# Attention's k^T v with four tokens of all heads on a partition: 40 matmuls of 128 rows in place of 72 of 64, for batches 3 to 7

## The chip, the cores and the metric

The kernel runs on one core of one Trainium2 chip. The metric is the device time of one execution in microseconds (us); the time of a kernel is the median of its runs. A profile of one execution goes with it. It shows five engines: PE (TensorE matmuls; its weight loads are listed as PEld), DVE (VectorE), ACT (ScalarE), POOL (GpSimd) and SP (SyncE, which here only issues DMAs). L237 means line 237 of the kernel before.

## The reference

Two stages follow each other, on 8 batches, 8 heads, 576 tokens and a head dimension of 64, all in float32.

```python
def phi(x, c, s):
    r = np.maximum(x, 0.0)
    return np.concatenate([r * c, r * s], axis=-1)      # 64 -> 128 features
q_p = phi(q, cos_w, sin_w)      # cos_w, sin_w depend on the token's position alone
k_p = phi(k, cos_w, sin_w)
kv = np.einsum('bhsf,bhsd->bhfd', k_p, v)               # 128 x 64 for each head
z = np.sum(k_p, axis=2)
num = np.einsum('bhsf,bhfd->bhsd', q_p, kv)
den = np.einsum('bhsf,bhf->bhs', q_p, z)[..., None] + 1e-06
x = num / den                                           # tokens x (8 heads * 64)
h = x @ w_in                                            # 512 -> 2048
g = h * (1.0 / (1.0 + np.exp(-1.702 * h)))
return g @ w_out                                        # 2048 -> 512
```

The matmuls run in bfloat16 with float32 sums.

## The kernel before

**The work of a batch.** From k and v the kernel forms k^T v for each head, a 128 x 65 matrix: 128 features by 64 columns of v and one column of ones, which gives the sum z of the denominator. q's features are transposed by DMA (L219) into qT. For each chunk of 128 tokens (the fifth has 64) eight matmuls, one a head, multiply qT with k^T v (`num_mm`, L310); DVE divides (`num_div`, L321 to L325), and a DMA transposes the quotient into x (L354). Then come 16 groups of four matmuls of 128 x 512 (`mm1`, L365), each group followed by a gelu on ScalarE (L371), and the product with w_out, written as seven Strassen-Winograd products of 16 matmuls each (`wino_mm`, L516). The last chunk of 64 tokens of each batch is left for a stage at the end.

**The layout of k and v.** `src_of` (L57) puts nine consecutive tokens on a partition and two heads above each other: 64 partitions hold one head's 576 tokens and the other 64 hold those of the next head, for four pairs of heads. A partition's piece in DRAM is 9 x 64 x 4 = 2304 bytes long, 512 such pieces a tensor. `load_kv` (L146) issues one DMA for k and one for v on SP.

`kv_operands` (L874) makes the matmul operands on DVE: for each of nine tokens two instructions (`trig`, L169: relu times cosine and relu times sine) on 128 x 256 elements, 18 in all, and from batch 3 on one cast of v to bfloat16 (`vcopy`, L193) on 128 x 2304.

The matmuls of k^T v (`kv_mm`, L232 to L238) contract the 64 partitions of one head, nine times with one token each:

```python
for i in range(i0, i1):                # pairs of heads
    for j in range(NS):                # NS = 9
        for hh in range(2):
            r = slice(hh * 64, hh * 64 + 64)
            nc.tensor.matmul(st["kv", i][:, hh, ds(col, n)], kr[r, j, i, :], rhs(r, i, j),
                             start=(j == 0), stop=(j == NS - 1))
```

That is 72 matmuls of 64 rows and 65 columns, alternating between the lower and the upper half of the array. `kv_evac` (L245) copies the result from PSUM to the tile kvs on DVE.

**q's layout.** From batch 1 on q is loaded differently (`load_chunks`, L127): four consecutive tokens of all eight heads on each of 128 partitions (pieces of 1024 bytes, 1024 of them) and the last 64 tokens on 64 partitions (512 pieces of 256 bytes), in two DMAs. `trig_q` (L176) makes each chunk's features with two instructions of 128 x 512, or 64 x 512 for the fifth chunk (L185).

**The order of the work.** All of it is written out by hand. In the loop at L886, block b runs batch b's `mm1` and Winograd products and prepares batch b + 1. At `fc` 0 DVE gets q's ten `trig_q` instructions and SP five transposes; at `fc` 1 `kv_operands` follows and SP issues the load of q of batch b + 2. At `fc` 12 DVE gets five sums for the Winograd products: two of s3 (L474), then s1, s2 and s4 (L470, L472, L476). At `fc` 14 PE does `kv_next` (L708): the 72 matmuls, and the eviction on DVE behind those sums. After `fc` 15 `x_next` (L880) runs chunk after chunk between the Winograd products. Once the fourth chunk's transpose is issued, SP gets `load_kv` for batch b + 2 (L933), and then the transpose of x's fifth chunk. Block 1 is arranged differently (its k^T v, for batch 2, comes after its `mm1`). GpSimd issues the DMAs of the output (L522), each of which waits for its sums on DVE or ACT. SP and GpSimd work through their lists in order.

**Borrowed places.** The batch 0 copy of v (`vb`) lies in the tile `sums`, and the end stage puts its sums into kr, kf, vf, qn and qf when these are done. The tile `warm` (zeros for matmuls that fill waits at the start) and `row` (batch 0's column sums) have places of their own.

Of the kernel before, what the change touches and what calls it, by code (L numbers as in the profile page):

```python
# [9 lines left out]
F32 = mybir.dt.float32  # L10
BF16 = mybir.dt.bfloat16
# [9 lines left out]
def kernel(  # L21
# [9 lines left out]
    nc = tc.nc  # L31
    B, H, S, D = q.shape
    d_model = H * D
    d_ff = moe_w_in.shape[1]
    KC = d_model // 128
    FC = d_ff // 128
    NS = S // 64
    MT = 512
    NI = H // 2

    const = ctx.enter_context(tc.tile_pool(name="const", bufs=1))
    one = ctx.enter_context(tc.tile_pool(name="one", bufs=1))
# [3 lines left out]
    small = ctx.enter_context(tc.tile_pool(name="small", bufs=3))  # L46
    pmm = ctx.enter_context(tc.tile_pool(name="pmm", bufs=4, space=PSUM))
    pat = ctx.enter_context(tc.tile_pool(name="pat", bufs=2, space=PSUM))
# [8 lines left out]
    def src_of(src, b, i0=0, i1=NI):  # L57
        return src[b, 2 * i0:2 * i1].rearrange("(i hh) (p j) d -> (hh p) i (j d)", hh=2, j=NS)

    qf = one.tile([128, 2560], F32, name="qf")  # L60
    kf, vf = [one.tile([128, NI, S], F32, name=n) for n in ("kf", "vf")]
    sums = one.tile([128, 4, d_ff], BF16, name="sums")
    vb = sums.rearrange("p n e -> p (n e)")[:, 0:NI * S].rearrange("p (i e) -> p i e", i=NI)
    qf0 = qf[:, 0:NI * S].rearrange("p (i e) -> p i e", i=NI)
    for t, src, cut in ((kf, k, 192), (qf0, q, 256)):
# [10 lines left out]
    nc.gpsimd.memset(ident, 1.0)  # L76
    nc.gpsimd.affine_select(out=ident, in_=ident, compare_op=mybir.AluOpType.is_equal,
                            fill=0.0, base=0, pattern=[[-1, 128]], channel_multiplier=1)
    warm = const.tile([128, 512], BF16)
    nc.vector.memset(warm, 0.0)  # L80
    pos_f = const.tile([128, NP], F32)
    nc.vector.tensor_copy(pos_f, pos_i)
# [22 lines left out]
    nc.scalar.activation(gl, halfpi, AF.Gelu_apprx_sigmoid)  # L105

    VW = 66
    wsum = one.tile([128, 4, d_ff], BF16, name="wsum")
    kr = one.tile([128, NS, NI, 128], BF16, name="kr")
    vt = one.tile([128, NS, NI, VW], BF16, name="vt")  # L110
    qn = one.tile([128, 5, H, 128], BF16, name="qn")
    qn0 = qn.rearrange("p c h f -> p (c h f)")[:, 0:NS * NI * 128].rearrange(
        "p (j i f) -> p j i f", j=NS, i=NI)
    qT = one.tile([128, H, 640], BF16, name="qT")
# [9 lines left out]
    def load(t, src, b, eng=nc.gpsimd):  # L124
        eng.dma_start(out=t, in_=src_of(src, b))

    def load_chunks(t, src, b, eng):  # L127
        eng.dma_start(out=t[:, 0:2048].rearrange("p (h e) -> p h e", h=H),
                      in_=src[b, :, 0:512, :].rearrange("h (p c) d -> p h (c d)", c=4))
        eng.dma_start(out=t[0:64, 2048:2560].rearrange("p (h e) -> p h e", h=H),  # L130
                      in_=src[b, :, 512:S, :].rearrange("h p d -> p h d"))

    def load_q(b, eng=nc.gpsimd):
        load_chunks(qf, q, b, eng)
# [5 lines left out]
    def wcol(kc, fc):  # L140
# [2 lines left out]
        w = w_in_t[g][:, kc, :] if g < 2 else w_in_t[2][:, kc, ts(g - 2, 512)]  # L143
        return w.rearrange("p (f c) -> p f c", c=4)[:, :, c]

    def load_kv(b):  # L146
        load(kf, k, b, nc.sync)
        load(vf, v, b, nc.sync)

    def load_wout(g):  # L150
        nc.gpsimd.dma_start(out=w_out_sb[:, ts(g, 4), :], in_=wout_r[g])
# [9 lines left out]
    def trig(dst, src, j, act=False, eng=nc.vector):  # L161

        i = src[:, :, ts(j, 64)]
        for cs, w in enumerate((cosw, sinw)):
            o = dst[:, j, :, ts(cs, 64)]
            if act is True or (act == "sin" and cs == 1):
                nc.scalar.activation(o, i, AF.Relu, scale=w[:, j:j + 1])
            else:
                eng.tensor_scalar(o, i, 0.0, w[:, j:j + 1], op0=MAX, op1=MUL)  # L169

    def chunk(t, c):
        if c < 4:
            return t[:, 0:2048].rearrange("p (h c d) -> p c h d", h=H, c=4)[:, c]
        return t[0:64, 2048:2560].rearrange("p (h d) -> p h d", h=H)

    def trig_q(c, act=False):  # L176
        n = 128 if c < 4 else 64
        i = chunk(qf, c)
        for cs, w in enumerate((cosw, sinw)):
            o = qn[0:n, c, :, ts(cs, 64)]  # L180
            sc = w[0:n, NS + c:NS + c + 1]
            if act:
                nc.scalar.activation(o, i, AF.Relu, scale=sc)
            else:
                nc.vector.tensor_scalar(o, i, 0.0, sc, op0=MAX, op1=MUL)  # L185

    def vcopy(i0=0, i1=NI, act=False):
        o = vt[:, :, i0:i1, 0:64].rearrange("p j i e -> p i j e")
        i = vf[:, i0:i1].rearrange("p i (j e) -> p i j e", e=64)
        if act:  # L190
            nc.scalar.activation(o, i, AF.Copy)
        else:
            nc.vector.tensor_copy(o, i)  # L193

    tps = {}

# [25 lines left out]
    st = {}  # L222
# [9 lines left out]
    def kv_mm(i0, i1, rhs, col, n):  # L232
        for i in range(i0, i1):
            for j in range(NS):
                for hh in range(2):
                    r = slice(hh * 64, hh * 64 + 64)
                    nc.tensor.matmul(st["kv", i][:, hh, ds(col, n)], kr[r, j, i, :], rhs(r, i, j),  # L237
                                     start=(j == 0), stop=(j == NS - 1))  # L238

    def kvs_of(h):  # L240
        return st["kvs"][:, h % 2, h // 2, 0:65]

    def kv_evac(i0, i1, n=65):
        o = st["kvs"][:, :, i0:i1, 0:n]
        nc.vector.tensor_copy(o, st["ps", i0].rearrange("p hh (i e) -> p hh i e", e=n))  # L245
# [6 lines left out]
                         start=first, stop=last)  # L252

    def ksum_rows():
        st["row"] = small.tile([2, 512], BF16, name="row", bufs=1)
        nc.vector.tensor_copy(st["row"], st["ks"][0:2])

    def ksum_turn():
# [27 lines left out]
    def div_half(a):  # L286
        pv = nums["ps"][a][:, 0:260].rearrange("p (h e) -> p h e", h=4)
        inv = small.tile([128, 4], F32, name="invh")
        nc.vector.reciprocal(inv, pv[:, :, 64])
        xn = small.tile([128, 4, 64], BF16, name="xh")  # L290
        nc.vector.tensor_tensor(xn, pv[:, :, 0:64],
                                inv.unsqueeze(2).to_broadcast([128, 4, 64]), op=MUL)
        nums[0, a] = [nums["ps"][a], xn]
# [79 lines left out]
    def mm1(b, fc):  # L373
        mm1_part(b, fc, 0, MT)
        gelu(fc)
# [78 lines left out]
    def tail_blk(i, qd):  # L454
# [1 line left out]
        return gt[:, ts(qd, 4), ts(i, 256)]  # L456

    tail_flat = [t.rearrange(f"p {r} -> p ({r})")[:, 0:2 * d_ff].rearrange("p (n f t) -> p n f t", n=2, f=HF)
                 for t, r in ((kr, "j i f"), (qT, "h t"))]
    tail_sg = {n: tail_flat[i // 2][:, i % 2] for i, n in enumerate(("s1", "s2", "s3", "s4"))}  # L460
    MAIN, TAIL = (main_blk, sg), (tail_blk, tail_sg)

# [130 lines left out]


    ws = {}
    for t, names in ((kf, ("s1", "s2")), (vf, ("s3", "s4"))):
        both = t.rearrange("p i e -> p (i e)")[:, 0:2048].bitcast(BF16).rearrange(
            "p (n k f) -> p n k f", n=2, k=2)
        for i, n in enumerate(names):
            ws[n] = both[:, i]  # L600
# [103 lines left out]
    def kv_mm_next():  # L704
        kv_open()
        kv_mm(0, 4, vt_rhs, 0, 65)

    def kv_next():  # L708
        kv_mm_next()
        kv_evac(0, 4)  # L710
# [161 lines left out]
    start_block(1)  # L872

    def kv_operands(b):  # L874
        for j in range(NS):
            trig(kr, kf, j, act="sin" if b == 2 and j % 2 else False)
        if b > 2:
            vcopy()

    def x_next(b, c):  # L880
        num_mm(c)
# [4 lines left out]
    for b in range(1, B):  # L886
        nb = b + 1 if b + 1 < B else None
        if nb is None:
            break
        f0 = 5 if b == 1 else 0  # L890
        for fc in range(f0, FC):
            if nb is not None and fc == f0:
                for c in range(5):
                    trig_q(c)
                    qturn_dma(c)
            if nb is not None and fc == f0 + 1 and b > 1:
                kv_operands(nb)

                if nb + 1 < B:
                    load_q(nb + 1, nc.sync)  # L900
            if fc == 8 and b == 1:
                load_q(nb + 1, nc.sync)
                g_sums(("s3",), 0)
                g_sums(("s3",), 1)
                kv_operands(nb)
            if fc == 12:
                if b > 1:
                    g_sums(("s3",), 0)
                    g_sums(("s3",), 1)
                g_sums(("s1", "s2", "s4") if b > 1 else ("s1", "s2"), 0)  # L910
            if fc == 13 and b == 1:
                vcopy()
            if fc == 14 and nb is not None and b > 1:
                kv_next()
            mm1(b, fc)
        if nb is not None:
            x_open(nb)
            if b > 1:
                x_next(nb, 0)
            g_sums(("s1", "s2"), 1)  # L920
            at = ({2 * p + 1: [p + 1 if nb < B - 1 else (4, 1, 2, 3)[p]] for p in range(4)} if b > 1 else
                  {3: [0], 4: [1], 5: [2], 6: [3], 8: [4]})
            wino_open()
            for p in range(7):
                for c in range(2):
                    wino_mm(p, c)
                    s = 2 * p + c
                    if c == 1:
                        wino_after(b, p)
                    for c2 in at.get(s, ()):  # L930
                        x_next(nb, c2)
                        if c2 == 3 and nb + 1 < B:
                            load_kv(nb + 1)  # L933
                    if s == 1 and b > 1:
                        g_sums(("s4",), 1)
                    if s == 1 and b == 1:
                        kv_mm_next()
                        kv_evac(0, 4)
                        g_sums(("s4",), 0)
                    if s == 6 and b == 1:  # L940
                        g_sums(("s4",), 1)
# [3 lines left out]
    b = B - 1  # L945
# [100 lines left out]
```

## Time and profile before

| what | us |
|---|---|
| median of 3 runs | 278.96 |
| the runs | 278.21, 278.96, 280.12 |
| the profiled execution | 281.36 |
| its span, first to last instruction | 279.6 |
| PE busy | 268.8 |
| DVE busy | 198.4 |
| ACT busy | 135.1 |
| POOL busy | 41.4 |

The granted clock of TensorE is 0.998 of full speed. Busy times of the engines lie beside each other and are not added up: an engine that isn't the one waited for costs nothing. Matmuls are pipelined: a matmul of 65 columns is listed with 0.19 us, but the next starts some 0.03 us behind it, so PE's time is read from the distance of starts. The DVE instructions overlap in the same way. Where a DMA is listed with a time to landing, it runs from the issue to the signal that all of it has arrived.

### The profile page before, as it was taken

What the parts mean: (1) busy time and instruction counts of PE and PEld (TensorE: products, weight loads), DVE (VectorE), ACT (ScalarE), POOL (GpSimd) and SP (SyncE); (2) the same over time, 40 slices, a digit from 0 to 9 for tenths busy, and PEclk for the clock granted to TensorE, in tenths of its full rate; (3) what the DMA queues carried; (4) which work ended last, traced back from release to release, by engine and by line L of the source; (5) the groups of instructions that cost most, each with busy time, mean ns of one, the idle gap of its engine ahead of it and who ended that gap; (6) DMA issues with size and microseconds to landing.
All of it is one profiled execution on the core that took longest, in us unless ns stands there. A gap on an engine that the chain in (4) does not pass through costs nothing.

```text
span 279.6 us, 6701 instructions
## 1 busy us (share of the span) xinstructions
PE 268.8 (96%) x2727; PEld 195.0 (70%) x2748; DVE 198.4 (71%) x474; ACT 135.1 (48%) x241; POOL 41.4 (15%) x70
## 2 busy tenths in 40 slices
PE   7899999997999999999999999999999999999994
PEld 2685645844885589558955896589657976899984
DVE  4943776469886985987598759876887783654741
ACT  6967552657116521662156215631464147577621
POOL 5690002300121001100220012001300130000320
PEclk9999999999999999999999999999999999999999
DMA  7999999999779998997699969997993340000233
GB/s 233 252 211 297 274 285 152 272 385 170 220 118 355 228 202 191 359 175 185 169 363 173 205 141 385 185 204 107 360 246 36 87 131 2 0 2 0 77 113 113
DMA packets 73661, 53.57 MB, mean 192 GB/s; under 512 B 52736, under 2 KB 63488, under 8 KB 73632
## 3 DMA queue, kind: packets, MB, share of 16 engines
q1 hardware_dynamic: 67504, 36.97, 58.4%
q0 software_dynamic: 6128, 16.19, 21.2%
q8 instruction: 21, 0.34, 0.5%
q14 instruction: 8, 0.07, 0.1%
HBM read 36.70 MB, written 9.44 MB: 165 GB/s over the span
## 4 chain that ended last, share of the span: by engine, by line
PE 77%; DVE 11%; DMA 8%; issue 1%; SPq 1%; ACT 1%; DVEq 0%
PE mm L516 29%; PE mm L365 24%; DMA kf<-in_k_dram 5%; PE mm L396 4%; PE mm L419 4%; DVE kr L169 4%; DMA qf<-in_q_dram 4%; PE mm L654 4%; PE at L516 3%; PE at L237 3%; PE at L310 3%; DVE qn L185 1%; DVE vt L193 1%; DVE sums L474 1%; PE mm L205 1%
## 5 line engine op out<-in xcount | busy, mean ns | idle before, releaser
L365 PE MATMUL mm<-xT,w_in 128*128 128x512 bf16 (+1 forms) x509 | 98.8, 344 | 3.2 <-ACT g L371 2.3
L365 PEld LDWEIGHTS <-w_in 128*128 128x128 bf16 x528 | 53.0, 113 | 42.7 <-issue 2.5
L371 ACT ACTIVATE g<-mm 128x512 bf16<-128x512 f32 x112 | 65.6, 598 | 33.1 <-PE mm L365 33.0
L516 PEld LDWEIGHTS <-sums 128*128 128x128 bf16 x448 | 42.4, 98 | 4.6
L522 POOL DMA_DIRECT2D out_dram<-ysb x24 | 17.4, 726 | 158.7 <-DVE den L321 79.0
L516 PE MATMUL mm<-wsum,sums 128*128 128x256 bf16 x336 | 40.1, 272 | 0.0
L516 PEld LDWEIGHTS <-g 128*128 128x128 bf16 x336 | 32.1, 98 | 3.8
L169 DVE TENSOR_SCALAR kr<-kf,cosw 128x256 bf16<-128x256 f32 x69 | 23.9, 351 | 7.8 <-DMA kf<-in_k_dram 7.8
L325 DVE TENSOR_TENSOR xn<-at,inv 128x512 bf16<-128x512 f32 x39 | 27.0, 691 | 1.3
L516 PE MATMUL mm<-w_out_sb,g 128*128 128x256 bf16 x224 | 26.6, 273 | 0.1
L169 DVE TENSOR_SCALAR kr<-kf,sinw 128x256 bf16<-128x256 f32 x64 | 21.8, 341 | 0.0
L185 DVE TENSOR_SCALAR qn<-qf,cosw 128x512 bf16<-128x512 f32 (+1 forms) x33 | 16.4, 498 | 7.0 <-DMA qf<-in_q_dram 7.0
L531 ACT ACTIVATE kept_p<-mm 128x512 f32<-128x512 f32 (+1 forms) x15 | 8.5, 570 | 19.5 <-PE mm L516 19.5
L583 ACT ACTIVATE ysb<-mm 128x512 f32<-128x512 f32 x6 | 3.6, 599 | 29.0 <-PE mm L516 29.0
L310 PEld LDWEIGHTS <-qT 128*128 128x128 bf16 x312 | 14.3, 97 | 3.0 <-issue 0.7
L321 DVE TENSOR_SCALAR den<-at 128x8 f32<-128x8 f32 x36 | 5.9, 163 | 14.8 <-PE at L310 14.8
L531 ACT ACTIVATE kept_u<-mm 128x512 f32<-128x512 f32 (+1 forms) x8 | 4.4, 544 | 24.6 <-DVE xn L325 16.8
L310 PE MATMUL at<-kvs,qT 128*128 128x65 bf16 x312 | 15.7, 193 | 0.5 <-DVE kvs L245 0.5
L185 DVE TENSOR_SCALAR qn<-qf,sinw 128x512 bf16<-128x512 f32 (+1 forms) x33 | 15.6, 474 | 0.0
L419 PE MATMUL mm<-w_out_sb,g 128*128 128x512 bf16 x62 | 14.7, 379 | 0.1
L516 PE MATMUL mm<-wsum,g 128*128 128x256 bf16 x112 | 13.4, 273 | 0.0
L516 PE MATMUL mm<-w_out_sb,sums 128*128 128x256 bf16 x112 | 13.4, 273 | 0.0
(147 smaller groups left out, 321.8 us busy)
## 6 DMA issues: line engine op xcount, KB each, us to landing
kf<-in_k_dram SPq DMA_DIRECT2D x6, 1152.0 KB, 6.6
vf<-in_v_dram SPq DMA_DIRECT2D x6, 1152.0 KB, 11.4
qf<-in_q_dram SPq DMA_DIRECT2D x6, 1024.0 KB, 7.3
out_dram<-ysb POOLq DMA_DIRECT2D x24, 256.0 KB, 6.6
w_out_sb<-in_moe_w_out_dram POOLq DMA_DIRECT2D x4, 512.0 KB, 17.6
kf<-in_k_dram POOLq DMA_DIRECT2D x1, 1152.0 KB, 13.3
vf<-in_v_dram POOLq DMA_DIRECT2D x1, 1152.0 KB, 20.7
w_in<-in_moe_w_in_dram POOLq DMA_DIRECT2D x2, 512.0 KB, 10.0
```

The source lines that it names most:

```text
L169: eng.tensor_scalar(o, i, 0.0, w[:, j:j + 1], op0=MAX, op1=MUL)
L185: nc.vector.tensor_scalar(o, i, 0.0, sc, op0=MAX, op1=MUL)
L310: nc.tensor.matmul(ps[:, h // 4, ds((h % 4) * 65, 65)], qT[:, h, ts(c, 128)], kvs_of(h), start=not eps_too, stop=(not eps_too or h % 4 == ...
L325: nc.vector.tensor_tensor(xn, pv[:, :, :, 0:64], inv.unsqueeze(3).to_broadcast([128, 2, 4, 64]), op=MUL)
L365: nc.tensor.matmul(hp[fc][:, t0:t1], wcol(kc, fc), x[b][:, kc, t0:t1], start=(kc == 0), stop=(kc == KC - 1))
L371: nc.scalar.activation(gT[fc // 4][:, fc % 4], hp.pop(fc), AF.Gelu_apprx_sigmoid)
L396: nc.tensor.matmul(hps[:, 64:B * 64], wcol(kc, fc), xt[:, kc, 64:B * 64], start=(kc == 0), stop=(kc == KC - 1))
L419: nc.tensor.matmul(yp[b, t, c0][:, c0:c1], w, w_out_sb[:, fc, c0:c1], start=(fc == 0), stop=(fc == FC - 1))
L516: nc.tensor.matmul(bank[to][c], lhs, rhs, start=opens, stop=(fc == HF - 1), skip_group_check=True)
L522: eng.dma_start(out=dst[:, 2 * i + c0:2 * i + c1, ts(n, HD)], in_=t[:, c0:c1])
L531: nc.scalar.activation(o, i, AF.Identity)
L654: nc.tensor.matmul(to[:, j], lhs, rhs, start=(opens and j == 0 and k == 0), stop=(k == 1), skip_group_check=True)
```

## The change

For batches 3 to 7 (`CB = 3`) k and v are loaded as q is, with `load_chunks`, so four DMAs in place of two are issued. Their operands are made chunk by chunk with `trig_q`, in ten instructions. v is cast in two instructions, one for the four full chunks and one for the fifth. The k^T v of a head is then five matmuls of 128 rows, one a chunk. In the fifth chunk the rows 64 to 127 of both operands are zeros, which GpSimd writes once, before batch 3's operands, with the column of ones. Batches 0 to 2 stay as they were.

The tiles grow to hold both layouts (kf and vf to 2560 elements, kr and vt to 5 x 8 rows), and as room is needed for that, `warm` and `row` move into the tile `wsum` and the tile `xh` gets two buffers in place of three.

```diff
-    kf, vf = [one.tile([128, NI, S], F32, name=n) for n in ("kf", "vf")]
+    kfc, vfc = [one.tile([128, 2560], F32, name=n) for n in ("kf", "vf")]
+    kf, vf = [t[:, 0:NI * S].rearrange("p (i e) -> p i e", i=NI) for t in (kfc, vfc)]
...
-    warm = const.tile([128, 512], BF16)
+    wsum = one.tile([128, 4, d_ff], BF16, name="wsum")
+    warm = wsum[:, 0, 0:512]
...
+    krc = one.tile([128, 5, H, 128], BF16, name="kr")
+    vtc = one.tile([128, 5, H, VW], BF16, name="vt")
...
     def load_kv(b):
-        load(kf, k, b, nc.sync)
-        load(vf, v, b, nc.sync)
+        if b < CB:
+            load(kf, k, b, nc.sync)
+            load(vf, v, b, nc.sync)
+        else:
+            load_chunks(kfc, k, b, nc.sync)
+            load_chunks(vfc, v, b, nc.sync)
...
+    def vcopy_chunks():
+        for c0, c1, n in ((0, 4, 128), (4, 5, 64)):
+            i = vfc[:, 0:2048] if c0 == 0 else vfc[0:64, 2048:2560]
+            nc.vector.tensor_copy(vtc[0:n, c0:c1, :, 0:64],
+                                  i.rearrange("p (h c d) -> p c h d", h=H, c=c1 - c0))
...
+    def kv_chunks():
+
+        t = pat.tile([128, 2, 512], F32, name="at")
+        for h in range(H):
+            for c in range(5):
+                nc.tensor.matmul(t[:, h // 4, ds((h % 4) * 65, 65)], krc[:, c, h, :],
+                                 vtc[:, c, h, 0:65], start=(c == 0), stop=(c == 4))
+        kvs = small.tile([128, 2, NI, VW], BF16, name="kvs", bufs=2)
+        nc.vector.tensor_copy(kvs[:, :, :, 0:65], t[:, :, 0:260].rearrange("p a (h e) -> p a h e", h=4))
+        st["kvs"], st["chunks"] = kvs, True
...
-        st["row"] = small.tile([2, 512], BF16, name="row", bufs=1)
+        st["row"] = wsum[0:2, 1, 0:512]
...
-        xn = small.tile([128, 4, 64], BF16, name="xh")
+        xn = small.tile([128, 4, 64], BF16, name="xh", bufs=2)
...
     def kv_operands(b):
+        if b >= CB:
+            if b == CB:
+                nc.gpsimd.memset(krc[64:128, 4], 0.0)
+                nc.gpsimd.memset(vtc[:, :, :, 64:66], 1.0)
+                nc.gpsimd.memset(vtc[64:128, 4], 0.0)
+            for c in range(5):
+                trig_q(c, dst=krc, src=kfc)
+            vcopy_chunks()
+            return
         for j in range(NS):
-            trig(kr, kf, j, act="sin" if b == 2 and j % 2 else False)
-        if b > 2:
-            vcopy()
+            trig(kr, kf, j, act="sin" if j % 2 else False)
...
             if fc == 14 and nb is not None and b > 1:
-                kv_next()
+                kv_chunks()
```

More of the change, by code (lines that the diff above doesn't have):

```diff
@@ L107 @@
     VW = 66
-    wsum = one.tile([128, 4, d_ff], BF16, name="wsum")
-    kr = one.tile([128, NS, NI, 128], BF16, name="kr")
-    vt = one.tile([128, NS, NI, VW], BF16, name="vt")
+    krc = one.tile([128, 5, H, 128], BF16, name="kr")
+    vtc = one.tile([128, 5, H, VW], BF16, name="vt")
+    kr, vt = [t.rearrange("p c h f -> p (c h f)")[:, 0:NS * NI * n].rearrange("p (j i f) -> p j i f", j=NS, i=NI)
+              for t, n in ((krc, 128), (vtc, VW))]
     qn = one.tile([128, 5, H, 128], BF16, name="qn")
@@ L144, in wcol @@
         return w.rearrange("p (f c) -> p f c", c=4)[:, :, c]
+    CB = 3
     def load_kv(b):
-        load(kf, k, b, nc.sync)
-        load(vf, v, b, nc.sync)
+        if b < CB:
[4 more added lines that the diff above has]
+            load_chunks(vfc, v, b, nc.sync)
     def load_wout(g):
@@ L174, in chunk, with trig_q @@
         return t[0:64, 2048:2560].rearrange("p (h d) -> p h d", h=H)
-    def trig_q(c, act=False):
+    def trig_q(c, act=False, dst=None, src=None):
         n = 128 if c < 4 else 64
-        i = chunk(qf, c)
+        i = chunk(qf if src is None else src, c)
         for cs, w in enumerate((cosw, sinw)):
-            o = qn[0:n, c, :, ts(cs, 64)]
+            o = (qn if dst is None else dst)[0:n, c, :, ts(cs, 64)]
             sc = w[0:n, NS + c:NS + c + 1]
@@ L238, in kv_mm @@
                                      start=(j == 0), stop=(j == NS - 1))
+    def kv_chunks():
[7 more added lines that the diff above has]
+        st["kvs"], st["chunks"] = kvs, True
     def kvs_of(h):
+        if "chunks" in st:
+            return st["kvs"][:, h // 4, h % 4, 0:65]
         return st["kvs"][:, h % 2, h // 2, 0:65]
@@ L458 @@
     tail_flat = [t.rearrange(f"p {r} -> p ({r})")[:, 0:2 * d_ff].rearrange("p (n f t) -> p n f t", n=2, f=HF)
-                 for t, r in ((kr, "j i f"), (qT, "h t"))]
+                 for t, r in ((krc, "c h f"), (qT, "h t"))]
     tail_sg = {n: tail_flat[i // 2][:, i % 2] for i, n in enumerate(("s1", "s2", "s3", "s4"))}
@@ L595 @@
     ws = {}
-    for t, names in ((kf, ("s1", "s2")), (vf, ("s3", "s4"))):
-        both = t.rearrange("p i e -> p (i e)")[:, 0:2048].bitcast(BF16).rearrange(
+    for t, names in ((kfc, ("s1", "s2")), (vfc, ("s3", "s4"))):
+        both = t[:, 0:2048].bitcast(BF16).rearrange(
             "p (n k f) -> p n k f", n=2, k=2)
```

## The prediction

> **What bounds the kernel now.** I read three views in this order: the chain of work that ended last, the busy time per block of the main loop, and the instructions in order of time where the two disagree. Times are microseconds from the start of the span unless marked ns.
>
> ```profile
> PE 77%; DVE 11%; DMA 8%; issue 1%; SPq 1%; ACT 1%; DVEq 0%
> ```
>
> The chain is mostly TensorE (PE). The question is whether that holds in the blocks that the change touches: the blocks of batches 2 to 6, each preparing the next batch's k^T v.
>
> ```profile
> 83.14:112.47 29.33, 28.72 (x288) 20.57 (x290) 23.12 (x57) 11.95 (x20) 3.06 (x5) 1.00 0.99 245
> 112.47:141.04 28.57, 28.41 (x287) 20.47 (x288) 23.05 (x57) 11.95 (x20) 2.90 (x5) 1.00 0.92 225
> ```
>
> The columns are the stretch, its length, then busy time of PE, weight loads, VectorE (DVE), ScalarE and GpSimd, the granted clock, the share of the DMA engines and GB/s. Blocks 3 to 6 take 28.57, 28.57, 28.57 and 28.56 with PE full: they are PE-bound. Block 2 takes 0.76 more. Its piece of the chain says why:
>
> ```profile
> 81.43 7.41 DMA kf<-in_k_dram
> 88.87 4.82 DVE kr L169 x18
> 93.69 1.27 DVE vt L193
> 94.96 1.20 DVE sums L474 x2
> 96.16 0.61 DVE sums L470
> 96.80 0.70 DVE sums L472
> 97.52 0.69 DVE sums L476
> 98.21 0.62 DVE kvs L245
> 98.88 0.40 PE at L310 x8
> ```
>
> In block 2 the load of batch 3's k lands late, all of DVE's work up to the eviction of k^T v (kvs) runs behind it, and the numerator matmuls of L310 start 0.83 after the matmul before them, where 0.216 is usual: PE stands for 0.61. So the change can act in two places: on PE in four full blocks, and on the load-and-DVE chain in block 2.
>
> **PE: 72 matmuls out, 40 in.** Removed are 36 pairs on 64 rows, added are 40 on 128 rows. Block 3 shows what the pairs cost, one instruction at a time (start, length, count):
>
> ```profile
> 124.18 0.38 PE L365 MATMUL mm<-xT,w_in 128*128 128x512 bf16 x1
> 124.49 1.26 PE L237 MATMUL at<-vt,kr 64*128 64x65 bf16 x72
> 125.69 0.41 PE L365 MATMUL mm<-xT,w_in 128*128 128x512 bf16 x1
> 127.44 0.41 PE L310 MATMUL at<-kvs,qT 128*128 128x65 bf16 x8
> ```
>
> The two matmuls of a pair start 3 to 4 ns apart and pairs follow at 29 to 30 ns, so a pair costs what one matmul of 65 columns costs. The first pair starts 0.312 after the last L365 (usual step: 0.216), and the next L365 starts 0.122 after the last pair, where the step behind L310 is 0.029: going to 64 rows and back costs some 0.19. It isn't the change of width, because L310, also 65 columns wide, starts a plain 0.216 after an L365. From 124.18 to 127.44 is 3.26. Afterwards this stretch holds one step of 0.216, 40 matmuls, and eight L365 steps of 0.216 (1.73). L310 is the nearest row: 128 rows, 65 columns, contiguous weights, eight in 0.24, or 30 ns each, so 40 take 1.20 and the stretch 3.14: 0.12 less. Bounds: at the best step of 29 ns, 0.15 less; at the pace of L388, 64 in 2.12 or 33 ns, nothing (0.01 more). L388 also accumulates, as the new ones do, but reads its weights with a stride (118 ns a load against 97 for L310's); the 64-row pairs accumulate and keep 29 ns, so I side with L310. Four blocks make **-0.48** (-0.60 to +0.04). Block 2 gains nothing here, because its PE waits for kvs anyway.
>
> The Trainium skill, "TensorEngine Tiling (Array Packing)", Tiling Modes (Key Properties), says that changing the tiling mode drains the TensorE; the 0.312 and 0.122 agree. The same page, Overview, gives two tiles of 64 rows up to twice the speed; counted in passes alone that speaks against the change, 40 in place of 36, four more at 30 ns, +0.12 a block; the rivals take it up.
>
> **DVE: k and v operands.** Rows by shape (count, busy, mean ns of one):
>
> ```profile
> L169 DVE TENSOR_SCALAR kr<-kf,cosw 128x256 bf16<-128x256 f32 x69 | 23.9, 351 | 7.8 <-DMA kf<-in_k_dram 7.8
> L185 DVE TENSOR_SCALAR qn<-qf,cosw 128x512 bf16<-128x512 f32 x27 | 13.6, 504 | 7.0 <-DMA qf<-in_q_dram 7.0
> L193 DVE CAST vt<-vf 128x2304 bf16<-128x2304 f32 x6 | 8.1, 1351 | 0.5 <-DMA vf<-in_v_dram 0.5
> ```
>
> They overlap, so I use steps. Removed: 18 of 128x256 from 88.87 to 93.60, 0.263 each, 4.73. Added: 10 in exactly q's layout, which take 4.09 in block 3 (111.37 to 115.46). The cast of v takes 1.27 and becomes two. From 2304 and 1152 elements (1351 and 761 ns) one element costs 0.51 ns, so the 2048-element part takes 1.14 and the 512-element part 0.34, 1.48 together. Net 0.43 less DVE work a batch. In blocks 3 to 6 that is worth nothing: PE hides it (in block 3 DVE even waits 0.76 on ScalarE behind the s3 sums). In block 2 it lies on the chain, if the data come in time. The kvs copy keeps its 520 elements.
>
> **DMA: two loads become four.** k and v take q's form: 1024 pieces of 1024 B and 512 of 256 B, in place of 512 of 2304 B. The trace's packet records give medians of 93 ns (2304 B), 46 (1024 B) and 18 (256 B). Over 16 engines a tensor goes from 512x93/16 = 2.98 to 1024x46/16 + 512x18/16 = 2.94 + 0.58: +0.54 a tensor, +1.09 for k and v, +1.24 at block 2's slower mean (106 ns for 93).
>
> ```profile
> kf<-in_k_dram SPq DMA_DIRECT2D x1, 1152.0 KB, 7.4
> vf<-in_v_dram SPq DMA_DIRECT2D x1, 1152.0 KB, 10.7
> qf<-in_q_dram SPq DMA_DIRECT2D x1, 1024.0 KB, 7.5
> qf<-in_q_dram SPq DMA_DIRECT2D x1, 128.0 KB, 6.2
> ```
>
> (Issue to landing in block 2; q's are the pair issued at 96.89.) The big part of k should land about where k did, 88.84: 2.94 against 2.98 of engine time. Its small part follows within 0.7, well before the fifth chunk needs it. v landed at 92.73; its parts then land at about 93.35 and 93.97. DVE: ten operands from 88.87 to 92.96, big cast 93.35 to 94.49, small cast to 94.83, where the old cast let go at 94.87. So block 2 gains **-0.04**: the DVE work saved is lost again to v's later landing. Bounds: -0.61 (the whole stall) to the late v among the rivals. In block 4, the tightest of the others (v landed there at 149.31 and DVE waited 0.50 for it), the casts end at 150.89 in place of 150.60; what follows can slip about 1.1 (0.18 ahead of the sums, 0.94 between kvs and L310, a little for the earlier PE).
>
> The Trainium skill, "DMA: Bandwidth & Descriptors", Why small descriptors are slow, puts a fixed 3 cycles on each packet, 11 for 256 B; by that the two loads grow by 8%, an estimate of +0.5. The trace has more: 18 ns for 256 B where a ninth of a 2304 B packet is 10. By the page, v would be nearly in time and the sum would be that of the chain rival below.
>
> **The queues.** SP issues two loads more a batch, some 0.6 each, more when many pieces are outstanding: the v load behind q and k in block 1 took 4.36 to issue. Behind them stand the transpose of x's last chunk (for the tail stage, not urgent), five q transposes and the next q load. Their data already queue behind v. If SP is held even until 88, the first q transpose lands by some 95.5 (1.37 for the x one, 1.3 and up to 4.8 for its own); L310 needs it at 98.4. Cost nothing; beyond 3 more it would show. GpSimd gets three memsets once, before batch 3's operands, behind the output issue that ends at 84.95. At a 128x512 memset's 0.52 they take about 1.03 + 0.17 + 0.53 = 1.7, so they end near 86.7, hidden by the wait for k until 88.87; even at twice that they precede the fifth chunk. GpSimd's next output issue is ten us later. The moved warm and row tiles are used before the w_out sums first write their place and add no work.
>
> **Sum.** -0.48 - 0.04 = -0.52. The profiled execution took 281.36, its span 279.60 and 1.76 around it; it stands 2.40 above the median of the three runs (278.96). I expect a span of 279.1 in an execution like it, and **278.4** as the median.
>
> **The rivals.**
> - The chain of block 2 shortens in full (chance 0.14). If v's big part lands by 92.96, the casts end at 94.44, 0.43 earlier, and the sum is -0.91: 278.0. For it: k's first half came in 4.0 where q's first 1024 pieces took 4.1 to 5.7, so the forms are close; against it: v is last in line behind 512 small packets, and 0.23 is all the room that was spare.
> - No gain on PE (0.17). At L388's 33 ns four blocks give +0.04, in sum 279.0; if the passes alone count and the 0.19 stays, +0.48 and 279.4 (page above). Against both: the rows of L310 and the pairs' pace.
> - Slower: v late in block 2 (0.22). Its place is the small cast, the new last arrival ahead of kvs. It decides when that cast ends 0.48 late, so when v's small part lands after 95.0, 2.3 behind v of before. An issue held 4.36 to about 87.6, with q's small part's worst landing of 10.7 (block 1), gives 98.3. Halfway between 94.0 and 98.3 the casts end at 96.5, 1.6 late; less 0.48 that is +1.1: 280.1. At the far end block 4 stalls too, past 282.
>
> **How the numbers follow.** Forecast 0.47 (278.0 to 278.8, by the PE bounds and a few tenths in block 2), the others as given. The three runs spread over 1.9, so a median moves by some 0.5 by itself. The range goes from 277.3, the chain rival with the full stall and that scatter, to 279.8, which leaves out the upper half of the late-v rival: about 0.17 outside. A change of 1% (2.8) is about what a measurement of this kernel can tell from none. Faster by more needs over twice the best case: 0.02. Slower by more needs v landing near 98 or stalls in several blocks: 0.06. Within 1%: 0.92.
>
> **What would show it.** Right: blocks 3 to 6 near 28.45; the step into and out of the 40 matmuls 0.216 and 0.03; ten DVE operands in 4.1; the wait ahead of the casts in block 2 on v. Wrong: steps of 33 ns inside the 40; blocks longer than 28.57, or L310 waiting for kvs in blocks 3 to 6; the wait of L310 in block 2 well off 0.6; DVE waiting on GpSimd's memsets.

## The result, and the profile after

The changed kernel takes 280.20 us (median of 22 runs, 278.96 to 283.26) against 279.07 for the kernel before (22 runs, 278.21 to 280.40): ratio 1.0042, 95% interval 1.0022 to 1.0062. It is slower, by some 1.2 us, where 0.5 less was forecast; the time lies 0.4 above the range. The ratio leaves out two runs of the changed kernel (283.23 and 283.26) that fell in a slower state of the chip.

The two first profiles don't say so by themselves: that of before is of an execution 2.3 above its median (281.36), that of after of one 1.2 below its own (278.96, span 277.0). The 2.3 are mostly one wait of 2.4 in block 1, ahead of everything that the change touches. So I compare stage by stage. Lines after the change are some 29 higher: L394 is `mm1`, L339 the numerators, L545 the Winograd products, L264 the copy to kvs.

The chain of after by engine, from the page:

```profile
PE 84%; DMA 6%; DVE 5%; ACT 1%; issue 1%; SPq 1%; DVEq 0%
```

Blocks 2 and 3 of after (stretch, length, busy times as in the prediction):

```profile
80.52:109.85 29.33, 28.52 (x255) 20.66 (x257) 23.62 (x50) 11.95 (x20) 5.02 (x8) 1.00 1.11 236
109.85:138.38 28.53, 28.37 (x256) 20.69 (x258) 22.48 (x50) 11.95 (x20) 2.91 (x5) 1.00 1.13 227
```

Block 3 falls from 28.57 to 28.52, and so do blocks 4 to 6. Measured like this, from the first `mm1` of a block to that of the next, block 2 took 29.17 and 29.85 in two profiles of before, and 29.33, 30.42 and 29.71 in three of after. (The prediction's 29.33 for before ends at 112.47, 0.16 behind the next block's first `mm1`; the excess of block 2 was 0.60 there, not 0.76, which is the 0.61 of the numerators' wait.) Its piece of the chain now starts with v:

```profile
79.62 11.24 DMA vf<-in_v_dram
90.88 1.55 DVE vt L208 x2
92.44 1.20 DVE sums L503 x2
...
95.69 0.62 DVE kvs L264
96.36 0.42 PE at L339 x8
```

k and its ten operands have left the chain: they were done at 89.1, and DVE stood for 1.78 until v came. The landings in that block (KB, issue to landing):

```profile
kf<-in_k_dram SPq DMA_DIRECT2D x1, 1024.0 KB, 6.7
vf<-in_v_dram SPq DMA_DIRECT2D x1, 1024.0 KB, 11.2
kf<-in_k_dram SPq DMA_DIRECT2D x1, 128.0 KB, 7.8
vf<-in_v_dram SPq DMA_DIRECT2D x1, 128.0 KB, 10.3
```

k's large load was issued at 78.37 and v's parts at 79.62 and 80.96, so v's parts land 12.5 and 12.9 after k's issue; all of v landed 11.3 after it before. In block 3 the 40 matmuls look like this:

```profile
121.51 0.59 PE L394 MATMUL mm<-xT,w_in 128*128 128x512 bf16 x2
121.94 1.37 PE L261 MATMUL at<-vt,kr 128*128 128x65 bf16 x40
123.14 1.89 PE L394 MATMUL mm<-xT,w_in 128*128 128x512 bf16 x7
124.87 0.42 PE L339 MATMUL at<-kvs,qT 128*128 128x65 bf16 x8
125.13 0.27 PE L545 MATMUL mm<-w_out_sb,g 128*128 128x256 bf16 x1
```

From the last `mm1` ahead of them (121.72, the second of the first line) to L339 it is 3.15, against 3.26 before: the switch between 64 and 128 rows is gone. But the eight L339 now take 0.26 to the next instruction (124.87 to 125.13), where the eight took 0.244.

### The profile page after: what moved, and what is told of

Its sections match the earlier page's. It is cut to its first block, busy times and chain, and to the rows that moved or that the text cites. A ratio compares the mean times of both kernels' runs of the same rounds, so it can differ in the third digit from the quotient of the medians.

```text
span 277.0 us, 6356 instructions
## 1 busy us (share of the span) xinstructions
PE 268.5 (97%) x2567; PEld 195.9 (71%) x2588; DVE 197.0 (71%) x439; ACT 135.1 (49%) x241; POOL 43.6 (16%) x73
## 4 chain that ended last, share of the span: by engine, by line
PE 84%; DMA 6%; DVE 5%; ACT 1%; issue 1%; SPq 1%; DVEq 0%
PE mm L545 30%; PE mm L394 29%; PE mm L448 5%; PE mm L425 4%; DMA vf<-in_v_dram 4%; PE mm L683 4%; PE at L545 3%; PE at L339 3%; DMA kf<-in_k_dram 2%; PE at L261 2%; PE at L253 1%; PE at L371 1%; DVE kr L179 1%; PE mm L221 1%; PE mm L417 1%
## 5 line engine op out<-in xcount | busy, mean ns | idle before, releaser
L394 PE MATMUL mm<-xT,w_in 128*128 128x512 bf16 (+1 forms) x509 | 98.6, 344 | 1.1
L394 PEld LDWEIGHTS <-w_in 128*128 128x128 bf16 x528 | 53.0, 113 | 40.3 <-issue 0.4
L545 PEld LDWEIGHTS <-sums 128*128 128x128 bf16 x448 | 42.5, 98 | 4.6
L545 PE MATMUL mm<-wsum,sums 128*128 128x256 bf16 x336 | 40.1, 272 | 0.0
L545 PEld LDWEIGHTS <-g 128*128 128x128 bf16 x336 | 32.1, 98 | 3.8
L545 PE MATMUL mm<-w_out_sb,g 128*128 128x256 bf16 x224 | 26.6, 272 | 0.1
L339 PEld LDWEIGHTS <-qT 128*128 128x128 bf16 x312 | 14.6, 98 | 3.2 <-issue 0.9
L195 DVE TENSOR_SCALAR qn<-qf,sinw 128x512 bf16<-128x512 f32 (+1 forms) x33 | 16.8, 509 | 0.0
L339 PE MATMUL at<-kvs,qT 128*128 128x65 bf16 x312 | 16.0, 193 | 0.6 <-DVE kvs L264 0.6
L545 PE MATMUL mm<-w_out_sb,sums 128*128 128x256 bf16 x112 | 13.4, 273 | 0.0
L545 PE MATMUL mm<-wsum,g 128*128 128x256 bf16 x112 | 13.4, 273 | 0.0
L208 DVE CAST vt<-vf 128x2048 bf16<-128x2048 f32 (+1 forms) x10 | 7.8, 820 | 6.6 <-DMA vf<-in_v_dram 6.6
L425 PE MATMUL mm<-xt,w_in 128*128 128x448 bf16 x64 | 12.3, 352 | 0.0
## 6 DMA issues: line engine op xcount, KB each, us to landing
vf<-in_v_dram SPq DMA_DIRECT2D x5, 1024.0 KB, 11.1
kf<-in_k_dram POOLq DMA_DIRECT2D x1, 1152.0 KB, 13.1
```

Source lines behind the costliest of these rows:

```text
L208: nc.vector.tensor_copy(vtc[0:n, c0:c1, :, 0:64], i.rearrange("p (h c d) -> p c h d", h=H, c=c1 - c0))
L339: nc.tensor.matmul(ps[:, h // 4, ds((h % 4) * 65, 65)], qT[:, h, ts(c, 128)], kvs_of(h), start=not eps_too, stop=(not eps_too or h % 4 == ...
L394: nc.tensor.matmul(hp[fc][:, t0:t1], wcol(kc, fc), x[b][:, kc, t0:t1], start=(kc == 0), stop=(kc == KC - 1))
L425: nc.tensor.matmul(hps[:, 64:B * 64], wcol(kc, fc), xt[:, kc, 64:B * 64], start=(kc == 0), stop=(kc == KC - 1))
L545: nc.tensor.matmul(bank[to][c], lhs, rhs, start=opens, stop=(fc == HF - 1), skip_group_check=True)
```

## The experiments

Two theories went in. L: the loads in small pieces bring v in late in block 2, and that costs more than PE gains. C, later P: the cost lies elsewhere, in the computation, in the other blocks, in GpSimd's zeros. Ratios are to the kernel before on the same chip, with 95% intervals.

**e1_after** and **e2_before**: both kernels again, unedited.

> The changed kernel, unchanged, for a profile of another execution and the ratio on the same chip as the others. Theory L (loads): the small pieces make v of batch 3 land late, more so in a typical execution than in the first profile; ratio 1.003 to 1.006, the numerators in block 2 start 1 to 3 us late against 0.8 in the first profile, and blocks 3 to 6 stay at 28.52. Theory C (computation): blocks 3 to 6 or the small sets of zeros on GpSimd cost what is missing; the wait in block 2 stays at 0.8 and the time stands elsewhere.

> The kernel before, for a profile of another execution. Its first profile was of an execution 2.3 us above its median, with one wait of 2.6 us in block 1. Both theories expect a ratio of 1.000, and if that wait is chance, a span near 277.3 with no such wait; the numerators of block 2 start 0.6 late again.

e1: 1.0040 (1.0014 to 1.0066); the numerators of block 2 start 1.04 later than usual, the 40 matmuls 0.65, and blocks 3 to 6 take 28.52. e2: 1.0016 (0.9991 to 1.0042), 0.92 late in block 2. Its wait in block 1 came again (2.4), so I was wrong to take it for chance in one profile. It hangs on the landing of batch 2's k; profiles of other versions have it anywhere from 0 to 3.0, and it is ahead of the change.

**e3_loads_only** and **e4_compute_only**: the change in two halves.

```diff
 # e3: operands and matmuls as before, on chunk loads
-            for c in range(5):
-                trig_q(c, dst=krc, src=kfc)
-            vcopy_chunks()
+        for j in range(NS):
+            trig(kr, kf, j, ...)
+        vcopy()
-                kv_chunks()
+                kv_next()
 # e4: loads as before, new operands and matmuls
-            load_chunks(kfc, k, b, nc.sync)
-            load_chunks(vfc, v, b, nc.sync)
+        load(kf, k, b, nc.sync)
+        load(vf, v, b, nc.sync)
```

> The loads alone: k and v of batches 3 to 7 come in by four DMAs in the new form, but the operands and the 72 matmuls are those of before and take the bytes as if they lay in the old form, so the results of these batches are not the reference's. Theory L: 1.004 to 1.008, slower than the changed kernel, as the 0.43 us less DVE work and the shorter matmuls are missing too; block 2 stands 1 to 1.5 us. Theory C: 1.000 to 1.002, only 1 us less of slack.

> The computation alone: ten operand instructions, two casts, 40 matmuls, but k and v of all batches still come in by two DMAs in the old form, so the results of batches 3 to 7 are not the reference's (and two more small sets of zeros on GpSimd). Theory L: 0.996 to 0.999, faster than before, with block 2's wait down to 0.2 to 0.4 and blocks 3 to 6 at 28.52. Theory C: 1.003 to 1.006, as slow as the changed kernel.

e3: 1.0046 (1.0012 to 1.0080), with block 2 at 30.03, 1.5 over a steady block, as L says; that it is slower than the changed kernel (1.0040), as L has it too, the intervals don't show. e4: 0.9987 (0.9960 to 1.0015). C falls: the loss comes with the loads. In e4 the numerators wait 0.54 in block 2, more than L's 0.2 to 0.4, because k sets the chain there.

**e5_after_early_k** and **e6_before_early_k**: only the place of batch 3's k load.

```diff
+            if b == 1:
+                load_k(nb + 1)          # start of block 1's Winograd products
...
-                            load_kv(nb + 1)
+                            if b > 1:
+                                load_k(nb + 1)
+                            load_v(nb + 1)
```

> The changed kernel, but batch 3's k is loaded at the start of block 1's Winograd products, ahead of x's transposes, and only its v where it was. Theory L (the loss is v landing late in block 2): v then has the queue for itself and lands some 4 us after the trigger of the old place, kvs is in time, block 2 comes down from 29.3 to 30.4 to some 28.6, and the ratio to the kernel before is 0.994 to 0.997. Rival P (the loss sits elsewhere, so before block 2 or in the end stage, and block 2 only shows chance): ratio 1.002 to 1.004. A third way: x's first transposes now wait behind k, and block 2 starts late by 1 or more.

> The kernel before with the same earlier load of batch 3's k. Theory L: block 2 comes down from 29.2 to 29.9 to some 28.6 too, ratio 0.996 to 0.999; against the changed kernel with the early k the steady blocks leave 0.05 a block in the change's favour. Rival P: the difference between these two kernels stays 0.4%, as between the kernels without the early load.

1.0196 (1.0162 to 1.0229) and 1.0073 (1.0048 to 1.0098): both far slower, and the third way that e5 names. In e6 block 2 is down to 28.57, without a wait. But x's first transpose queues behind k; from e5's chain of waits:

```profile
74.22 9.32 DMA xT<-xn
```

The fifth chunk's quotient needs the first one's buffer (there are four) and DVE stops until that transpose has landed; the last Winograd matmuls of block 1 start 2.2 (e6) and 4.7 (e5) after those before them. That transpose landed 6.85 after its issue in e6 and 9.32 in e5, where k's small load stands ahead of it as well; e5 also has the new computation, which the pair doesn't separate. This place has no room for a load of k, and the pair doesn't decide between L and P.

**e7_no_small** and **e10_no_small_batch_3**: the small loads left out, for all batches or for batch 3 alone.

```diff
-            load_chunks(kfc, k, b, nc.sync)
-            load_chunks(vfc, v, b, nc.sync)
+            load_chunks(kfc, k, b, nc.sync, small=False)      # e10: small=b > CB
+            load_chunks(vfc, v, b, nc.sync, small=False)
```

> The changed kernel without the two small loads of k and v (the last 64 tokens of batches 3 to 7 are left out of the loads, stale data is used in their place, so these results are not the reference's). If the 512 pieces of 256 B a tensor are what the loads cost, v lands 1.1 to 1.3 us earlier in block 2 and the ratio falls from 1.004 to 0.998 to 1.001. If it is the 1024 B form of the large part, v stays where it was and the ratio at 1.003 to 1.004.

> The changed kernel without the two small loads for batch 3 alone (stale data stands in for its last 64 tokens, so batch 3's results are not the reference's); batches 4 to 7 load theirs. Theory L: v of batch 3 lands 1.2 to 1.6 us earlier after the issue of k, and the ratio is that of the kernel without any small loads, 0.997 to 1.000. Rival P: four fifths of the loss stay, 1.002 to 1.004.

e7: 0.9984 (0.9967 to 1.0001), e10: 1.0009 (0.9984 to 1.0035). The 1024 B pieces cost nothing that shows; the two small loads carry the loss. By e10's median most of it goes with batch 3's alone, though its interval reaches 1.0035. GpSimd's zeros and the moved tiles are in both kernels, so they aren't the cause. v's large load lands at 11.9 (e7) and 11.6 (e10) after k's issue, 12.5 to 13.1 in the kernels with both small loads (table below).

**e8_kvs_order**: heads in PSUM and kvs in the order of before.

```diff
-                nc.tensor.matmul(t[:, h // 4, ds((h % 4) * 65, 65)], krc[:, c, h, :],
+                nc.tensor.matmul(t[:, h % 2, ds((h // 2) * 65, 65)], krc[:, c, h, :],
```

> The changed kernel, but the heads lie in kvs and in PSUM in the order of before (even heads in one bank, odd heads in the other). Blocks 3 to 6 gained 0.05 where the 40 matmuls alone gained 0.11; the eight numerator matmuls of a chunk take 0.256 in place of 0.244. If the order of kvs does that, the eight are back at 0.244 and the blocks fall from 28.52 to 28.46; if it is where the tiles lie, both stay. The time itself, 1.002 to 1.004, can't tell.

1.0048 (1.0016 to 1.0081), as slow as the change. Blocks 3 to 6 take 28.46, 28.47, 28.46, 28.47, and the eight are back at 0.24 (126.81 to 127.05):

```profile
126.81 0.41 PE L337 MATMUL at<-kvs,qT 128*128 128x65 bf16 x8
127.05 0.49 PE L543 MATMUL mm<-w_out_sb,g 128*128 128x256 bf16 x3
```

**e9_from_batch_4**: `CB = 4`, so that batch 3 stays in the old form.

> The changed kernel with the new form from batch 4 on, so batch 3 is loaded and computed as before (and GpSimd's zeros come a block later). Theory L, the whole loss in block 2: blocks 3 to 5 keep their 0.05 each, nothing else is lost, ratio 0.997 to 1.001. Rival P, loss in every block or elsewhere: about four fifths of it stays, ratio 1.002 to 1.004.

1.0009 (0.9979 to 1.0040): the median says, as L does, that most of the loss is gone with batch 3 alone, but the interval still holds P's 1.002 to 1.004. The dose in e14 and the load chains below are the firmer ground for L.

**e11_early_small** and **e12_early_small_order**: batch 3's small loads ahead of x's transposes; e12 with e8's edit.

```diff
+            if b == 1:
+                load_chunks(kfc, k, CB, nc.sync, big=False)
+                load_chunks(vfc, v, CB, nc.sync, big=False)
```

> The changed kernel with batch 3's two small loads issued at the start of block 1's Winograd products; the large ones stay where they were. They are 1.2 us of DMA work ahead of x's first transpose, where a whole load of k was too much. Theory L: block 2 as without small loads, ratio 0.997 to 1.000, if x's transposes stay in time; if they don't, block 2 starts late by up to 1 and the ratio is 1.001 to 1.003. Rival P: 1.003 to 1.004.

> The same with kvs in the order of before. Theory L: four blocks of 28.46, so 0.2 us less than the kernel with the early small loads, ratio 0.996 to 0.999, the first version below the kernel before. If block 1 suffers, 1.000 to 1.002.

1.0011 (0.9977 to 1.0045) and 1.0002 (0.9976 to 1.0028). In e11's profile block 2 has no wait at all (28.52), but block 1 has one of 1.7 for x's transpose, as in e5. What is won in one block is partly paid in the other. Neither beats the kernel before.

**e13_from_4_order**, **e14_more_small**, **e15_after**: e9 with e8's edit; a double dose of small loads; the change again.

```diff
 # e14, between k's loads and v's, for batch 3
+                for i, src in ((0, k), (8, v)):
+                    nc.sync.dma_start(out=gt[0:64, i:i + 8, 64:192].bitcast(F32),
+                                      in_=src[b, :, 512:S, :].rearrange("h p d -> p h d"))
```

> The new form from batch 4 on, and kvs in the order of before: block 2 as before, blocks 3 to 6 at 28.46 (28.52 where batch 3's k^T v in the old form is used), 0.3 to 0.4 us less in all, ratio 0.997 to 1.000. If the ratio stays at 1.001, the untraced executions lose something that the profiles don't show.

> The changed kernel with two further small loads for batch 3 (copies of the last 64 tokens of k and v, to a place that nothing reads then) between k's loads and v's. They are 1.2 us of DMA time ahead of v. If the time follows block 2's load chain, kvs comes 1.2 to 1.5 later after the issue of k than in the changed kernel (17.2 to 17.8), so 18.5 to 19.3, and the ratio rises by 0.004 to 0.005 above e15's. If the loss is elsewhere, block 2 has slack in most executions and the ratio rises by less than 0.002.

> The changed kernel once more, on the same chip as e13 and e14: 1.003 to 1.005.

e13: 0.9981 (0.9948 to 1.0015), the best of all, but not told from no change; blocks 3 to 6 at 28.46. e15: 1.0031 (1.0007 to 1.0056). e14: 1.0112 (1.0061 to 1.0163), 0.0081 or 2.3 us above e15. The time follows the load chain, though the dose was twice what I had worked out. The casts of after, of e14 and of e10 (DVE idle ahead of them in brackets):

```profile
90.88 1.55 DVE L208 CAST vt<-vf 128x2048 bf16<-128x2048 f32 x2 [1.78 <-DMA vf<-in_v_dram]
```

```profile
94.68 1.55 DVE L212 CAST vt<-vf 128x2048 bf16<-128x2048 f32 x2 [3.27 <-DMA vf<-in_v_dram]
```

```profile
90.87 1.55 DVE L210 CAST vt<-vf 128x2048 bf16<-128x2048 f32 x2 [0.53 <-DMA vf<-in_v_dram]
```

All of block 2's chains together, in us after the issue of batch 3's k:

| small loads in this place | kernels | v's large load landed | copy to kvs starts |
|---|---|---|---|
| old form (2304 B) | before, e2, e9, e13 | 11.3, 11.9, 11.5, 11.7 | 16.70, 17.18, 16.79, 16.81 |
| old form, new computation | e4 | 11.6 | 16.37 |
| none | e7, e10, e11, e12 | 11.9, 11.6, 11.6, 11.4 | 16.98, 16.31, 16.50, 16.17 |
| two | after, e1, e8, e15 | 12.5, 13.0, 13.1, 12.8 | 17.24, 17.68, 17.82, 17.51 |
| two, old computation | e3 | 12.5 | 17.65 |
| four | e14 | 15.7 | 20.49 |

## Why the prediction was wrong

**The step that failed: from DMA work to landing.** I added the mean engine time of the small pieces, 0.62 a tensor at block 2's slower mean, to v's old landing, as if all engines were through together. The packets were priced rightly: k's small load shows 512 packets of 18 ns in every profile. But a load counts as landed when its last part is in, and that came later than the mean. From the packet records, in us after the issue of batch 3's k:

| small loads | kernels | 98% of k's and v's large packets done | the last one | v's large load landed |
|---|---|---|---|---|
| old form | before, e2, e9 | 10.3, 10.8, 10.5 | 10.8, 11.4, 11.0 | 11.3, 11.9, 11.5 |
| none | e7, e10, e12 | 10.6, 10.3, 10.3 | 11.4, 11.1, 10.8 | 11.9, 11.6, 11.4 |
| two | after, e1, e15, e8 | 10.8, 10.7, 10.6, 11.1 | 11.3, 12.3, 11.9, 12.2 | 12.5, 13.0, 12.8, 13.1 |
| four | e14 | 13.6 | 14.8 | 15.7 |

With two small loads the bulk of the data is 0.4 later than with none, near the 0.58 of k's small load; the last 2% and the signal behind them add 0.8, so that v lands 1.2 later.

The trace also holds the signals of a landing: 16 for each load, as many as there are DMA engines, and I read each as one engine's. Of those of v's large load the eighth came at 11.63, 11.29, 11.79 and 11.29 (after, e1, e8, e15), no later than the 11.9 that I had, and the last at 12.49, 12.92, 13.07 and 12.76. By that reading half of the engines were in time, and the slowest ones made the landing. In six profiles without the two small loads (before, e2, e9, e13, e7, e10) v's 16 signals come within 0.06 of each other, at 11.2 to 11.9; what bunches them there isn't shown.

SP's issue doesn't explain it. v's large load was issued later, 1.25 to 1.35 after k's in place of 0.59, and 4.33 in e14. But that issue was over at 2.0 to 2.6 (5.95 in e14), and by the count of packets v's first one moved at 6.4 to 6.8 (8.78 in e14): the load stood in the queue by then.

Why the slowest fall behind isn't shown. In the last stretch, from 10 us after k's issue to v's landing, 256 B packets (v's small load and the transposes) last 38 to 60 ns on average where both small loads are, and 31 to 44 where none is, which is no clear mark. The engines are full with and without them: the packets that start between 0.9 after the issue and the landing take 12.73 of 16 engines' time in e15, in a stretch of 11.86, and 10.97 in e10, in 10.66 (packets overlap).

Why the dose isn't linear isn't shown either: in e14 two more loads, 1.2 by my price, hold up even the bulk by 2.8. Between the last of k's large packets and the first of v's (98% of the one to 2% of the other) lie 0.14 to 0.20 without small loads, 0.5 to 1.2 with two and 2.68 in e14. In these 2.68 small packets take 1.16 of 16 engines' time, at 19 ns each, and packets of 4096 B from GpSimd's queue (the output) another 1.50.

By the Trainium skill, "DMA: Bandwidth & Descriptors", Why small descriptors are slow, which has a fixed cost for each packet, my estimate was +0.5 for the loads as a whole, with v nearly in time. The landings here, 1.2 to 1.7 later, are far from it.

**What followed from it.** v's parts landed 12.5 to 13.1 and 12.9 to 13.5 after k's issue, where I had 11.9 and 12.5. The casts ended at 14.0 to 14.6 in place of 13.4 to 13.9, and kvs started at 17.56 on average against 16.87: **+0.7, where -0.04 was forecast**. The late-v rival (0.22) came true, with its place off: I put it on the small cast as last arrival, but the large cast, held by k's small load ahead of it, already ends so late that the small one only follows. That this rival's 280.1 lies next to the measured 280.20 is chance: it had the casts 1.6 late, where they were 0.7, and PE's gain at 0.48, where it was 0.2.

**PE.** The stretch with the 40 matmuls takes 3.15, as forecast (3.14), at 30.2 ns each: siding with L310's pace against L388's was right. Only half of it reached the block, 0.05 in place of 0.12, so four blocks gave 0.2 and not 0.48. What I missed is that the change also reorders kvs, whose copy I dismissed because its size stays; five chunks at 0.012 take 0.06 back, and e8 returned it.

**Right:** the ten operands (85.06 to 89.1, 4.0), the casts (1.55 busy), k's large part (6.7 to 7.6 against 7.4), nothing lost to SP, though v's small load took 2.2 to 3.9 to issue (my 4.8 for a q transpose was too low: the first one behind the loads took 9.9 in before and 6.0 to 6.4 in after, e1 and e15, still in time), and all of the casts' delay hidden in blocks 3 to 6. One sign of being wrong came without a cost: DVE did wait on GpSimd's zeros (last section).

**What stays open.** By the profiles the sum is +0.7 - 0.2 and +0.1 in the end stage (53.1 against 53.0, not explained), so +0.6, or 1.002. Measured are 1.0042, 1.0040 and 1.0031. The intervals reach down to 1.0022, 1.0014 and 1.0007; whether 0.3 to 0.6 us more sit in executions without a profile, perhaps in block 2, or are scatter, these runs don't settle.

Block 2's excess over a steady block is 0.6, 1.3, 0.4 and 0.9 in the four profiles with the old form and the old computation there (before, e2, e9, e13) and 0.8, 1.9, 1.2 and 1.3 in four with the change (after, e1, e15, e8): 0.5 more on average, with a scatter of about 1. The spans of whole profiles can't help: block 1's wait of 2.4 happened to fall in those of before and e2 and not in those of after, e1 and e15.

## What to carry to other kernels

A load has landed when its slowest part is in: where the queue was full, mean packet time gave the bulk, and the landing was off by more than as much again (0.4 for the bulk, 1.2 for the landing), so leave more than that as slack or as range. What is saved on the bound engine is worth nothing in the one stage that waits for a load, and a new layout's extra pieces land just there. When a tensor changes its order, cost its readers too, even if their count and size stay.

## What the runs showed of the hardware

Row tiling (two tiles of 64 rows) has a price at its edges: 0.096 on the way to 64 rows (a step of 0.312 for 0.216) and 0.093 on the way back (0.122 for 0.029). A pair of 64 rows, at 30.5 ns on average, costs what one matmul of 128 rows does, at 30.2.

The place of a small matmul's operand shows: eight numerator matmuls take 0.244 with the heads of kvs in even and odd halves and 0.256 with them in sequence (e8).

GpSimd's zeros held DVE up. In after, the columns as before:

```profile
82.39 1.07 POOL L906 MEMSET kr<- 64x1024 bf16 x1
82.49 1.25 DVE L195 TENSOR_SCALAR qn<-qf,sinw 128x512 bf16<-128x512 f32 x1
83.52 0.34 POOL L907 MEMSET vt<- 128x80 bf16 x1
83.67 0.47 DVE L195 TENSOR_SCALAR qn<-qf,cosw 64x512 bf16<-64x512 f32 x1
83.92 0.70 POOL L908 MEMSET vt<- 64x528 bf16 x1
84.06 0.83 DVE L195 TENSOR_SCALAR qn<-qf,sinw 64x512 bf16<-64x512 f32 x1
```

A DVE instruction that usually takes 0.47 takes 1.25 when a memset starts 0.10 ahead of it and ends only after the memset (83.74 against 83.46), and 0.83 beside the third; beside the second and shortest it keeps its 0.47. The Trainium skill, "SBUF — State Buffer", Who interferes with whom, has the two engines share a port pair, which one instruction holds to its end when DVE works in a two-port mode. The two long lines agree; which mode these instructions ran in, no run here shows. It cost nothing, since DVE then waited for k, for 0.17 in this profile.
